# Graph hops and attention: the edge counts of the front moved ahead of the first table and onto TensorE

## The chip, the cores and the metric

The kernel runs on one core of one Trainium2 chip. The metric is the device time of one execution in microseconds, lower is better. The engines are named as the profile names them: PE is TensorE (PEld its weight loads), DVE is VectorE, ACT is ScalarE, POOL is GpSimd, SP is SyncE, which here only issues DMAs. PSUM is the memory that PE accumulates into; DVE and ACT read it back.

## The reference, cut to what matters

There are N = 10000 nodes with D = 128 features and E = 160000 edges. Seven times the features are spread along the edges; then each node attends over its eight versions of itself.

```python
h = x
toks = [x]
for _ in range(7):
    msg = h[src] * deg_inv_sqrt[src, None] * deg_inv_sqrt[dst, None]
    h = segment_sum(msg, dst, N)
    toks.append(h)
tok = jnp.stack(toks, axis=1)          # (N, 8, D)
# layernorm, q/k/v, softmax over the 8 tokens, wo, residual,
# layernorm, softmax of r @ w_r over the tokens, weighted sum -> (N, D)
```

The graph comes as two unsorted lists of edge ends, `src` and `dst`. Before a hop can be done with matmuls, the edges must be sorted into blocks of destination nodes. That sorting, and the first scaled table of node features, is the front of the kernel, and it is what the change touches.

## The kernel before, in words

**Order of the whole.** `Hops.run` (L525) calls `first_table` (L162), `pass_a` (L231) and `decode` (L286), then builds the matrices of the blocks while it does the first hop, does the six further hops, and the attention follows. A scheduler places the instructions: each engine executes its own list in a fixed order, and the list is not always the order of the source. Engines wait for each other by semaphores only.

**The first table.** `first_table` loads x (5.1 MB) with DMAs issued by ACT (L170, L171) into the buffer `tab` number 1, multiplies 79 tiles of rows by 1/sqrt(degree) on ACT (L173), takes the largest magnitude of all of it with one DVE reduction `mc` (L176), finds a power of two from it through a small chain of PE and DVE steps (`pow2`, `colmax`, `spread`), and writes table 0 as two 16-bit halves: the high half on ACT (L152) and the rest on DVE (L153), in four pieces of 20 tiles. Each piece is stored to DRAM.

**Sorting by destination block.** `pass_a` lays the 160000 edges out as 128 partitions x 1250 columns. `key` is the destination's block (dst >> 7, 79 values), `d1` and `d2` hold the other digits of the edge. The columns are 25 chunks of B = 50. Inside a chunk each edge needs its rank among the edges of its partition with the same key. `lag` (L213) counts, for each edge, the equal keys ahead of it in its chunk: for each distance l from 1 to 49 one DVE comparison writes `eq` (L219) and one DVE addition adds it to `wl` (L220), so the 98 instructions depend on each other in a chain through `wl` and one `eq` buffer.

Then for each chunk: `oh`, a one-hot of the keys (DVE, L189); `U`, 50 matmuls that count the keys of the partitions before (PE, L263); `U2`, its copy (ACT, L270); `ux` = oh x U2 (DVE, L202); `R`, 17 matmuls that pick out the offsets and add `wl` (PE, L206 and L207); `rk`, the rank (DVE, L210); `o12`, two products of oh with d1 and d2 (DVE, L195; the trace shortens the name to `o`, and `oh`, `rob` and `R` of other places also come from L189 and L195); `ro`, a one-hot of the ranks (DVE, L278); `ta`, 50 matmuls that put the edges' values in their place (PE, L283); and `TT`, the sum of ta's two halves (DVE, L284). `oh`, `U2`, `rk` and `ro` have two buffers, `U`, `R` and `ta` two in PSUM, `ux` and `o12` one. `count` for the next chunk is called before the rank of this one, so `oh` and `U` run one chunk ahead.

**Decoding.** `decode` unpacks TT into keys, sources and destinations with DVE and ACT operations on 128 x 2000 elements, scales TT on DVE (L307), and `lag_rows` (L222) counts equal keys `kB` again, now along the 25 chunks: 24 comparisons (L228) and 24 additions to `wB` (L229). After that `place` begins the next sorting step with two one-hots, `ur` matmuls (L336) and their copies.

Of the kernel before, what the change touches and what calls it, by code (L numbers as in the profile page):

```python
# [7 lines left out]
F32 = mybir.dt.float32  # L8
F16 = mybir.dt.float16
# [4 lines left out]
ALU = mybir.AluOpType  # L14
# [23 lines left out]
class Hops:  # L38
    def __init__(self, ctx, dp, missing, tc, x, src, dst, dis):
# [36 lines left out]
        V.memset(self.ones16, 1.0)  # L76
        self.iof = cp.tile([128, 128], F32, name="iof")
# [84 lines left out]
    def first_table(self):  # L162
        nc, V, A = self.nc, self.nc.vector, self.nc.scalar
        tab0 = self.tab[0]
        y = self.tab[1].bitcast(F32)
        nc.gpsimd.memset(y[:, NT - 1:, :], 0.0)
        nc.gpsimd.memset(tab0[:, NT:, :], 0.0)
        h = NT // 2
        for a, b in ((0, h), (h, NT - 1)):
            nc.scalar.dma_start(y[:, a:b, :], self.x[a * 128:b * 128, :].rearrange("(t p) d -> p t d", p=128))  # L170
        nc.scalar.dma_start(y[:N - (NT - 1) * 128, NT - 1, :], self.x[(NT - 1) * 128:, :])  # L171
        for t in range(NT):
            A.activation(y[:, t, :], y[:, t, :], AF.Copy, scale=self.disT[:, t:t + 1])  # L173
        with self.tc.tile_pool(name="ft", bufs=1) as sp, self.tc.tile_pool(name="ftp", bufs=1, space=PSUM) as pp:
            mc = sp.tile([128, 1], F32, name="mc")
            V.tensor_reduce(mc, y[:, :NT, :], axis=mybir.AxisListType.XY, op=ALU.max, apply_absolute_value=True)  # L176
            q = self.pow2(pp, sp, mc, 2.0 ** 40)
            V.tensor_copy(self.sinv, q[:, 1:2])
            for a in range(0, NT, 20):
                b = min(NT, a + 20)  # L180
                self.to_table(y[:, a:b, :], tab0, q[:, 0:1], a, b)
                self.rows(0, tab0, a, b, nc.sync)
        V.tensor_scalar(self.ctok[0], self.disT, self.sinv, None, op0=ALU.mult)
# [29 lines left out]
    def lag(self, ep, key, w, a, m):  # L213

        V = self.nc.vector
        V.memset(w, 0.0)
        for l in range(1, m):
            eq = ep.tile([128, a, m], F16, name="eq")
            V.tensor_tensor(eq[:, :, l:], key[:, :, l:], key[:, :, :m - l], op=ALU.is_equal)  # L219
            V.tensor_add(w[:, :, l:], w[:, :, l:], eq[:, :, l:])  # L220

    def lag_rows(self, ep, key, w, m):  # L222

        V = self.nc.vector
        V.memset(w, 0.0)
        for l in range(1, m):
            eq = ep.tile(list(key.shape), F16, name="eq")
            V.tensor_tensor(eq[:, l:], key[:, l:], key[:, :m - l], op=ALU.is_equal)  # L228
            V.tensor_add(w[:, l:], w[:, l:], eq[:, l:])  # L229

    def pass_a(self):  # L231
        tc, nc, V, A, T, G = self.tc, self.nc, self.nc.vector, self.nc.scalar, self.nc.tensor, self.nc.gpsimd
        with ExitStack() as c:
# [5 lines left out]
            with tc.tile_pool(name="pe", bufs=1) as ep:  # L239
# [12 lines left out]
                self.lag(ep, key.rearrange("p (c b) -> p c b", b=B), wl, NCH, B)  # L252
# [12 lines left out]

            st = count(0)
            for ch in range(NCH):
                oh, U = st
                U2 = wp.tile([128, NK, 2], F16, name="U2")
                A.activation(U2, U[:, :, None].to_broadcast([128, NK, 2]), AF.Copy)  # L270
                if ch + 1 < NCH:
# [7 lines left out]
                                self.io2[:, None].to_broadcast([128, NP, 128, 2]), op=ALU.is_equal)  # L279
                ta = pp.tile([128, 2, NK], F32, name="ta")  # L280
# [3 lines left out]
                V.tensor_reduce(self.TT[:, ch, :NK], ta.rearrange("p h k -> p k h"), axis=X, op=ALU.add)  # L284

    def decode(self):  # L286
# [3 lines left out]
        with tc.tile_pool(name="pd", bufs=1) as ep:  # L290
# [16 lines left out]
            V.tensor_scalar(self.TT, self.TT, 1024.0, -1023.0, op0=ALU.mult, op1=ALU.add)  # L307
            self.lag_rows(ep, self.kB, self.wB, NCH)
# [216 lines left out]
    def run(self, ctx, nhop=K):  # L525
        tc, nc, V, A, T, G = self.tc, self.nc, self.nc.vector, self.nc.scalar, self.nc.tensor, self.nc.gpsimd
        with ExitStack() as c:
# [3 lines left out]
            self.first_table()  # L531
# [626 lines left out]
```

## Time and profile before

| | us |
|---|---|
| median of 3 runs | 4419.87 (4418.78 to 4421.31) |
| the profiled execution | 4388.44 |
| its span, from first to last record | 4386.5 |
| busy: PE, DVE, ACT, POOL | 3836.6, 3383.4, 2453.6, 1680.0 |
| mean granted PE clock | 0.963 |

The profile is of one execution. Its own time is 31.4 us under the median of the runs, so its span and the median are not compared with each other; a difference between two profiles is compared with a difference between two medians. The front takes the first 560 us of the span. In the answers that list stretches of time, a row gives the stretch, its length, the busy time of PE, PEld, DVE, ACT and POOL with the number of instructions, then the granted PE clock (1.00 is full speed), the busy share of the DMA engines and GB/s. In the rows of the timeline the numbers are the start, the time that the group covers, the engine, the line, the operation, what is written and from what, and how many; in brackets stands how long the engine had been idle before, and what ended that.

### The profile page before, as it was taken

The numbers are of one execution on the slowest core, as the hardware profiler recorded it, in microseconds if no ns is written. First come the engines' busy times: TensorE is split into PE (matmuls) and PEld (weight loads), VectorE is DVE, ScalarE is ACT, GpSimd is POOL, SyncE is SP. The second block draws the span as 40 slices with busy tenths as digits, with TensorE's granted clock in tenths as the row PEclk, the third lists the DMA queues.
The fourth block names the chain that finished last, engine by engine and source line by source line (L and its number), as shares of the span: only waits on it lengthen the run. The fifth ranks groups of instructions, "written<-read, shape, count | busy, mean of one in ns | idle before, by whom it ended". The sixth has DMA issues, their size and how long they took to land.

```text
span 4386.5 us, 162053 instructions
## 1 busy us (share of the span) xinstructions
PE 3836.6 (87%) x69456; PEld 3003.0 (68%) x69456; DVE 3383.4 (77%) x6923; ACT 2453.6 (56%) x5989; POOL 1680.0 (38%) x1898
## 2 busy tenths in 40 slices
PE   0466379999997999999999999999999998999997
PEld 0466366666665777777777777777777776788875
DVE  5888899999995677666666666666765554899998
ACT  3000036666565666566566656656665555988885
POOL 0000023333333555555455545545555553222222
PEclk9887689999998999999999999999999998999998
DMA  4000034444445555555555555555555555122220
GB/s 122 1 1 1 1 108 152 149 153 149 143 155 180 182 181 188 170 184 183 175 184 179 184 173 184 181 176 180 183 185 167 170 170 151 54 78 78 77 72 19
DMA packets 320607, 594.73 MB, mean 136 GB/s; under 512 B 55623, under 2 KB 213541, under 8 KB 314629
## 3 DMA queue, kind: packets, MB, share of 16 engines
q1 hardware_dynamic: 219749, 477.37, 34.1%
q0 software_dynamic: 35392, 72.55, 5.4%
q10 hardware_dynamic: 64736, 34.38, 2.8%
q8 instruction: 544, 8.91, 0.8%
q14 instruction: 186, 1.52, 0.1%
HBM read 455.43 MB, written 128.67 MB: 133 GB/s over the span
## 4 chain that ended last, share of the span: by engine, by line
PE 56%; ACT 6%; DVE 3%; issue 1%; DMA 1%; SPq 0%; another core or an unknown queue 0%; ACTq 0%; DVEq 0%; POOLq 0%
PE acc L468 21%; PE p L492 20%; ACT eb L495 5%; PE acc L454 3%; PE pv L842 3%; PE po L853 3%; PE pu L831 3%; PE pt L821 1%; DVE eb L495 1%; PE ps L873 1%; PE pf L1021 1%; PE sm L879 1%; DMA og<-tabh,oidx 1%; DVE st L948 0%; SPq L734 0%
## 5 line engine op out<-in xcount | busy, mean ns | idle before, releaser
L495 ACT CAST eb<-p 128x512 f16<-128x512 f32 x3081 | 1598.5, 600 | 935.5 <-PE p L492 878.9
L495 DVE CAST eb<-p 128x512 f16<-128x512 f32 x1896 | 1180.7, 683 | 570.9 <-PE p L492 531.4
L492 PE MATMUL p<-tab,w 128*32 128x256 f16 x39816 | 1437.7, 275 | 111.1 <-ACT eb L495 35.1
L492 PEld LDWEIGHTS <-w 128*32 128x32 fp8e4 x39816 | 974.1, 96 | 491.4 <-issue 400.7
L468 PE MATMUL acc<-eb,w 128*128 128x256 f16 (+1 forms) x9954 | 1244.5, 274 | 13.1 <-DVE indeg L544 8.8
L439 POOL DMA_INDIRECT og<-tabh,oidx x553 | 631.9, 1143 | 1628.7 <-PE acc L454 868.7
L468 PEld LDWEIGHTS <-w 128*128 128x128 fp8e4 x9954 | 954.6, 98 | 174.6 <-issue 59.6
L439 POOL DMA_INDIRECT og<-tabd,oidx x541 | 557.4, 1030 | 457.5 <-PE acc L481 276.3
L521 POOL TENSOR_SCALAR r<-s,ctok 128x128 f32<-128x128 f32 x474 | 297.4, 627 | 40.0 <-DVE s L483 25.5
L627 DVE SCALAR_TENSOR_TENSOR tab<-s,c,tab 128x128 f16<-128x128 f32 x395 | 140.8, 356 | 183.1 <-ACT tab L626 182.1
L626 ACT ACTIVATE tab<-s,c 128x128 f16<-128x128 f32 x395 | 158.6, 401 | 166.0 <-DVE s L483 157.5
L483 DVE TENSOR_REDUCE s<-acc 128x128 f32<-128x256 f32 x553 | 228.5, 413 | 25.4 <-PE acc L481 18.8
L867 ACT ACTIVATE junk<-x 128x128 f32<-128x128 f32 x625 | 245.0, 394 | 0.0
L270 ACT ACTIVATE U<-U 128x158 f16<-128x158 f32 x25 | 7.6, 303 | 378.6 <-PE U L263 378.6
L429 DVE TENSOR_TENSOR w<-dsl,iof 128x2432 fp8e4<-128x2432 f16 x79 | 211.8, 2681 | 0.0
L283 PE MATMUL ta<-o,ro 128*128 128x158 f16 x1250 | 127.2, 278 | 90.5 <-DVE ro L278 90.5
L853 PEld LDWEIGHTS po<-v,pT 128*128 128x128 f32 x1250 | 160.1, 194 | 43.7 <-issue 26.7
L283 PEld LDWEIGHTS <-ro 128*128 128x128 f16 x1250 | 122.1, 119 | 94.5 <-DVE ro L278 94.2
L842 PE MATMUL pv<-Wv,xT 128*128 128x131 f32 x1250 | 175.6, 284 | 3.7 <-ACT xT L822 3.1
L853 PE MATMUL po<-v,pT 128*128 128x128 f32 x1250 | 167.7, 278 | 7.0 <-DVE o L859 7.0
L925 POOL TENSOR_TENSOR p<-e,in 128x512 f32<-128x512 f32 (+1 forms) x40 | 40.8, 1021 | 342.0 <-DVE e L923 342.0
L842 PEld LDWEIGHTS pv<-Wv,xT 128*128 128x128 f32 x1250 | 153.3, 192 | 20.2 <-issue 8.3
(267 smaller groups left out, 4509.1 us busy)
## 6 DMA issues: line engine op xcount, KB each, us to landing
w<-gsd SPq DMA_DIRECT2D x474, 592.0 KB
gsd<-w SPq DMA_DIRECT2D x79, 592.0 KB
rb<-srow SPq DMA_DIRECT2D x79, 576.0 KB
tok<-r SPq DMA_DIRECT2D x546, 64.0 KB
x<-tok SPq DMA_DIRECT2D x266, 128.0 KB
tabd<-tab ACTq DMA_DIRECT2D x395, 64.0 KB
og<-tabh,oidx POOLq DMA_INDIRECT x553
og<-tabd,oidx POOLq DMA_INDIRECT x541
```

The lines of the kernel that those rows point to most:

```text
L283: T.matmul(ta, ro[:, j, :, i], o12[:, j, :, i], start=j + i == 0, stop=j + i == NP)
L429: V.tensor_tensor(w[:, :NJ * 128].rearrange("p (j d) -> p j d", d=128), dsl[:, g, :, None].to_broadcast([128, NJ, 128]), self.iof1[:, None ...
L439: self.nc.gpsimd.indirect_dma_start(out=o, out_offset=None, in_=src[0] if i == NI else src[1], in_offset=bass.IndirectOffsetOnAxis(ap=self ...
L468: T.matmul(acc[0][:, :m], w[:, J * 128:(J + 1) * 128], e[:, j, :m], start=first and J == 0, stop=J == NG - 1 and not (first or late))
L483: V.tensor_reduce(s, acc[0][:, 0:256].rearrange("p (h d) -> p d h", h=2), axis=X, op=ALU.add)
L492: T.matmul(p[32 * q:32 * q + 32, j], w[:, NJ * 128 + s * CAP:NJ * 128 + (s + 1) * CAP], tab[:, s, :], start=True, stop=True)
L495: (A.copy if evac(jj) else V.tensor_copy)(e[:, :n, 0:256], p[:, :n].rearrange("p j h d -> p j (h d)"))
L521: self.nc.gpsimd.tensor_scalar(r, s, ct[:, t:t + 1], None, op0=ALU.mult)
L626: A.activation(new[:, t, 0:128], s, AF.Copy, scale=c1[:, t:t + 1])
L842: T.matmul(p[:, g - a, :], S[i]["xT"][:, g, :], Wv, start=True, stop=True)
L853: T.matmul(p[:, g - a, :], PT[i % 2][:, g, :], S[i]["v"][:, g, :128], start=True, stop=True)
L867: A.activation(j, S[i]["x"][:, g, :], AF.Square, bias=S[i]["x"][:, g, 0:1], scale=-1.0, accum_out=S[i]["sq"][:, g:g + 1])
```

## The change

The change is in the front alone.

- `first_table` is split. `first_rows` (loading x, scaling its rows) is now called inside `pass_a`, behind the unpacking of the edges; the rest of `first_table` (reduction, power of two, table 0, stores) is called when the loop over chunks comes to chunk 2.
- `lag` and `lag_rows` no longer add on DVE. DVE only compares, into three rotating `eq` buffers. PE adds: a matmul with the identity `id16` as weights adds each `eq` to a sum `W` in PSUM (one to three, or up to five, banks; a first matmul with zeros clears each), and ACT copies `W` to `wl` or `wB` at the end.
- The sum `TT` of a chunk is issued one chunk later (`take(ch - 1, ta)`), after the next chunk's `rk` and `ro` in the source.
- TT's scaling in `decode` goes from DVE to ACT.

```diff
+        self.zero16 = cp.tile([128, 512], F16, name="zero16")
+        V.memset(self.zero16, 0.0)
...
-    def first_table(self):
+    def first_rows(self):
...
         for t in range(NT):
             A.activation(y[:, t, :], y[:, t, :], AF.Copy, scale=self.disT[:, t:t + 1])
+
+    def first_table(self):
+        nc, V = self.nc, self.nc.vector
+        tab0, y = self.tab[0], self.tab[1].bitcast(F32)
         with self.tc.tile_pool(name="ft", bufs=1) as sp, self.tc.tile_pool(name="ftp", bufs=1, space=PSUM) as pp:
...
-    def lag(self, ep, key, w, a, m):
+    def lag(self, ep, pp, key, w, a, m):
-        V = self.nc.vector
-        V.memset(w, 0.0)
+        V, T, n = self.nc.vector, self.nc.tensor, 512 // m
+        W = pp.tile([128, -(-a // n), 512], F32, name="W")
+        parts = [(b, b * n, min(a, b * n + n)) for b in range(W.shape[1])]
+        out = lambda b, r: W[:, b, :r * m].rearrange("p (a m) -> p a m", m=m)
+        for b, r, e in parts:
+            T.matmul(W[:, b, :(e - r) * m], self.id16, self.zero16[:, :(e - r) * m], start=True, stop=False, skip_group_check=True)
         for l in range(1, m):
             eq = ep.tile([128, a, m], F16, name="eq")
             V.tensor_tensor(eq[:, :, l:], key[:, :, l:], key[:, :, :m - l], op=ALU.is_equal)
-            V.tensor_add(w[:, :, l:], w[:, :, l:], eq[:, :, l:])
+            for b, r, e in parts:
+                T.matmul(out(b, e - r)[:, :, l:], self.id16, eq[:, r:e, l:], start=False, stop=l == m - 1, skip_group_check=True)
+        for b, r, e in parts:
+            self.nc.scalar.copy(w[:, r:e, :], out(b, e - r))
...
-    def lag_rows(self, ep, key, w, m):
+    def lag_rows(self, ep, pp, key, w, m):
...
             V.tensor_tensor(eq[:, l:], key[:, l:], key[:, :m - l], op=ALU.is_equal)
-            V.tensor_add(w[:, l:], w[:, l:], eq[:, l:])
+            for b, r, e in parts:
+                r1 = max(r, l * k)
+                if r1 < e:
+                    T.matmul(W[:, b, r1 - r:e - r], self.id16, flat(eq)[:, r1:e], start=False, stop=(l + 1) * k >= e,
+                             skip_group_check=True)
+        for b, r, e in parts:
+            self.nc.scalar.copy(flat(w)[:, r:e], W[:, b, :e - r])
...
-            with tc.tile_pool(name="pe", bufs=1) as ep:
+            with tc.tile_pool(name="pe", bufs=1) as ep, tc.tile_pool(name="peq", bufs=3) as eqp, \
+                    tc.tile_pool(name="pW", bufs=1, space=PSUM) as pw:
...
-                self.lag(ep, key.rearrange("p (c b) -> p c b", b=B), wl, NCH, B)
+                self.first_rows()
+                self.lag(eqp, pw, key.rearrange("p (c b) -> p c b", b=B), wl, NCH, B)
...
+            def take(ch, ta):
+                V.tensor_reduce(self.TT[:, ch, :NK], ta.rearrange("p h k -> p k h"), axis=X, op=ALU.add)
+
             st = count(0)
             for ch in range(NCH):
+                if ch == 2:
+                    self.first_table()
...
+                if ch:
+                    take(ch - 1, ta)
                 ta = pp.tile([128, 2, NK], F32, name="ta")
...
-                V.tensor_reduce(self.TT[:, ch, :NK], ta.rearrange("p h k -> p k h"), axis=X, op=ALU.add)
+            take(NCH - 1, ta)
...
-            V.tensor_scalar(self.TT, self.TT, 1024.0, -1023.0, op0=ALU.mult, op1=ALU.add)
-            self.lag_rows(ep, self.kB, self.wB, NCH)
+            A.activation(self.TT, self.TT, AF.Copy, scale=1024.0, bias=-1023.0)
+            self.lag_rows(eqp, pw, self.kB, self.wB, NCH)
...
-            self.first_table()
             self.pass_a()
```

The scheduler moves more than the source shows. Rows below are in the order in which an engine executes them; a row names the line, the operation, the tile written, the tiles read, and the size; line numbers are each kernel's own (an operation at L219 before stands at L229 after).

First place: DVE's list around the reduction `mc` of the first table (`m`, `r` and `q` are the small chain to the power of two, `tab_230` and `tab_231` tables 0 and 1). Before, first the middle of the table's chain and then the start of the count:

```order
L147 TENSOR_SCALAR q_359<-q_359 128x1
L178 COPY sinv<-q_359 128x1
L183 TENSOR_SCALAR ctok_235<-disT,sinv 128x79
L153 SCALAR_TENSOR_TENSOR tab_230<-tab_231,q_359,tab_230 128x20x128 x3
L153 SCALAR_TENSOR_TENSOR tab_230<-tab_231,q_359,tab_230 128x19x128
L216 MEMSET wl 128x625
L249 TENSOR_SCALAR it<-ed 128x1250
L219 TENSOR_TENSOR eq<-key 128x25x49
L250 TENSOR_TENSOR it<-it 128x1250
L220 TENSOR_TENSOR wl<-wl,eq 128x25x49
```

Now, the end of the count and what follows it on DVE (`tab_233` is table 1):

```order
L229 TENSOR_TENSOR eq<-key 128x25x2
L229 TENSOR_TENSOR eq<-key 128x25
L195 TENSOR_TENSOR oh<-key,io_214 128x3950 x2
L201 TENSOR_TENSOR o_766<-oh,d_264 128x25x158
L201 TENSOR_TENSOR o_766<-oh,d_265 128x25x158
L182 TENSOR_REDUCE mc<-tab_233 128x1
L208 TENSOR_TENSOR ux<-oh,U_689 128x3950
L127 TENSOR_REDUCE m_966<-pm 1x1
L195 TENSOR_TENSOR oh<-key,io_214 128x3950
L143 TENSOR_SCALAR r_968<-m_966 1x1
```

The whole count and two chunks' `oh` with one chunk's products now stand ahead of `mc`, and the chain behind it is mixed with the chunks 0 to 2.

Second place: DVE's list in the middle of the loop over chunks. Before, one of the two patterns that take turns there:

```order
L278 TENSOR_TENSOR ro<-rk,io_212 128x6400
L189 TENSOR_TENSOR oh<-key,io_212 128x3950
L202 TENSOR_TENSOR ux<-oh,U_882 128x3950
L284 TENSOR_REDUCE TT<-ta 128x79
L195 TENSOR_TENSOR o_959<-oh,d_385 128x25x158
L195 TENSOR_TENSOR o_959<-oh,d_386 128x25x158
L210 TENSOR_REDUCE rk<-R 128x50
```

Now, the same in every chunk:

```order
L309 TENSOR_TENSOR ro<-rk,io_214 128x6400
L195 TENSOR_TENSOR oh<-key,io_214 128x3950
L208 TENSOR_TENSOR ux<-oh,U_1397 128x3950
L201 TENSOR_TENSOR o_1474<-oh,d_264 128x25x158
L201 TENSOR_TENSOR o_1474<-oh,d_265 128x25x158
L216 TENSOR_REDUCE rk<-R 128x50
L293 TENSOR_REDUCE TT<-ta 128x79
```

`TT` stood between `ro` and the products; it now stands behind `rk`. In its place the first product waits for the last `ta` matmul of the chunk before, because `o12` has one buffer. PE's list is now, chunk by chunk, `ta`, `U`, `R`.

Third place: the head of ACT's list (`tab_231` before and `tab_233` now are table 1, `U_614` and `U_689` the first U2). Before:

```order
L170 DMA tab_231<-in_x 128x39x128 x2
L171 DMA tab_231<-in_x 16x128
L173 ACT_TABLE_LOAD
L173 ACTIVATE tab_231<-tab_231,disT 128x128 x79
L152 ACTIVATE tab_230<-tab_231,q_359 128x20x128 x3
```

Now:

```order
L172 DMA tab_233<-in_x 128x39x128
L270 ACT_TABLE_LOAD
L270 CAST key<-it 128x1250
L172 DMA tab_233<-in_x 128x39x128
L272 ACTIVATE d_264<-it 128x1250
L173 DMA tab_233<-in_x 16x128
L175 ACTIVATE tab_233<-tab_233,disT 128x128 x5
L276 ACTIVATE d_265<-it 128x1250
L175 ACTIVATE tab_233<-tab_233,disT 128x128 x74
L233 CAST wl<-W 128x500 x2
```

The key is made between the two large DMAs of x, and the copies of `W` stand behind all 79 scalings. From the first one-hot of `place` on, every engine's list is the same as before, and POOL's and SP's lists are the same from the first row.

More of the change, by code (lines that the diff above doesn't have):

```diff
@@ L160, in rows @@
             eng.dma_start(o.rearrange("(t p) w -> p t w", p=128), tab[:, a:t1, :])
-    def first_table(self):
-        nc, V, A = self.nc, self.nc.vector, self.nc.scalar
+    def first_rows(self):
+        nc, A = self.nc, self.nc.scalar
         tab0 = self.tab[0]
@@ L219, in lag @@
             V.tensor_tensor(eq[:, :, l:], key[:, :, l:], key[:, :, :m - l], op=ALU.is_equal)
-            V.tensor_add(w[:, :, l:], w[:, :, l:], eq[:, :, l:])
-    def lag_rows(self, ep, key, w, m):
-        V = self.nc.vector
-        V.memset(w, 0.0)
+            for b, r, e in parts:
[3 more added lines that the diff above has]
+    def lag_rows(self, ep, pp, key, w, m):
+        V, T, k = self.nc.vector, self.nc.tensor, key.shape[2]
+        n = 512 // k * k
+        W = pp.tile([128, -(-m * k // n), 512], F32, name="W")
+        flat = lambda z: z.rearrange("p m k -> p (m k)")
+        parts = [(b, b * n, min(m * k, b * n + n)) for b in range(W.shape[1])]
+        for b, r, e in parts:
+            T.matmul(W[:, b, :e - r], self.id16, self.zero16[:, :e - r], start=True, stop=False, skip_group_check=True)
         for l in range(1, m):
@@ L228, in lag_rows @@
             V.tensor_tensor(eq[:, l:], key[:, l:], key[:, :m - l], op=ALU.is_equal)
-            V.tensor_add(w[:, l:], w[:, l:], eq[:, l:])
+            for b, r, e in parts:
[3 more added lines that the diff above has]
+                             skip_group_check=True)
+        for b, r, e in parts:
+            self.nc.scalar.copy(flat(w)[:, r:e], W[:, b, :e - r])
     def pass_a(self):
@@ L289, in decode @@
         self.kB, self.sl, self.dl, self.wB = (bp.tile([128, NCH, NTP], F16, name=n) for n in ("kB", "sl", "dl", "wB"))
-        with tc.tile_pool(name="pd", bufs=1) as ep:
+        with tc.tile_pool(name="pd", bufs=1) as ep, tc.tile_pool(name="pdq", bufs=3) as eqp, \
+                tc.tile_pool(name="pdW", bufs=1, space=PSUM) as pw:
             vi = ep.tile([128, NCH, NTP], I32, name="vi")
```

## The prediction

> **What bounds the kernel now.** I read the span and the engines' busy times first, then stretches of the front, then what DVE waited for, then the timeline where a term needed a duration. Stretches: total length, then busy PE, PEld, DVE, ACT, POOL, then clock.
>
> ```profile
> span 4386.5 us, 162053 instructions
> ...
> 0.00:76.90 76.90, 1.32 (x4) 0.76 (x4) 32.41 (x47) 36.05 (x88) 5.23 (x24) 1.00 0.44 134
> 76.90:130.98 54.08, 0.00 (x0) 0.00 (x0) 50.68 (x100) 1.74 (x2) 0.00 (x0) 1.00 0.19 56
> 130.98:500.04 369.06, 236.16 (x2925) 221.63 (x2925) 313.88 (x175) 7.57 (x25) 0.00 (x0) 0.81 0.00 1
> 500.04:513.40 13.36, 0.00 (x0) 0.00 (x0) 13.29 (x11) 3.74 (x2) 0.00 (x0) 0.56 0.00 0
> 513.40:547.69 34.29, 0.00 (x0) 0.00 (x0) 32.57 (x50) 0.00 (x0) 0.00 (x0) 0.50 0.00 0
> 547.69:560.24 12.55, 6.90 (x46) 5.69 (x47) 6.74 (x4) 0.57 (x2) 0.00 (x0) 0.65 0.00 0
> 560.24:4386.50 3826.26, 3592.18 (x66481) 2774.94 (x66480) 2933.82 (x6540) 2403.92 (x5871) 1674.77 (x1874) 0.98 0.48 152
> ```
>
> The six stretches of the front are: first table; count of equal keys; 25 chunks; decoding; second count; start of `place`. From 76.90 on DVE is busy nearly all the time or waits for PE. In both counts PE does nothing, so 54.08 and 34.29 us are pure DVE chains. After 560 us PE is busy 94% of the time; every engine's list from the start of `place` on is unchanged, so I take what the front saves as a shift of all that follows.
>
> What DVE waits for, in total, times, longest:
>
> ```profile
> DVE mc L176 <- ACT tab L173: 33.5, 1, 33.5
> ...
> DVE TT L284 <- PE ta L283: 55.2, 25, 5.9
> ```
>
> DVE sits idle 33.5 us for ACT to scale x, and 55.2 us in the chunks for `ta`. These two and the additions are what the change is aimed at.
>
> ```profile
> L219 DVE TENSOR_TENSOR eq<-key 128x1225 f16<-128x1225 f16 (+48 forms) x49 | 24.8, 505 | 1.7
> L220 DVE TENSOR_TENSOR wl<-wl,eq 128x1225 f16<-128x1225 f16 (+48 forms) x49 | 24.5, 501 | 1.6
> L228 DVE TENSOR_TENSOR eq<-kB 128x1920 f16<-128x1920 f16 (+23 forms) x24 | 16.3, 678 | 0.8
> L153 DVE SCALAR_TENSOR_TENSOR tab<-tab,q,tab 128x2560 f16<-128x2560 f32 (+1 forms) x4 | 11.1, 2847 | 1.9 <-ACT tab L152 1.9
> ```
>
> **The front up to the last chunk.** I follow DVE's new list in time.
>
> ```profile
> 2.19 12.61 ACTq L170 DMA_DIRECT2D tab<-in_x  x1
> 6.31 0.81 DVE L244 TENSOR_SCALAR it<-ed 128x1250 int32<-128x1250 int32 x1 [5.17 <-DMA ed<-in_dst]
> 13.77 0.89 DVE L225 MEMSET wB<- 128x1000 uint32 x1 [0.28 <-DVE triw L72]
> 24.95 23.17 ACT L173 ACTIVATE tab<-tab,disT 128x128 f32<-128x128 f32 x79
> 48.16 10.69 DVE L176 TENSOR_REDUCE mc<-tab 128x1 f32<-128x10112 f32 x1 [33.45 <-ACT tab L173]
> 76.15 1.24 ACT L247 ACTIVATE d<-it 128x1250 f16<-128x1250 int32 x1
> 77.74 1.45 DVE L250 TENSOR_TENSOR it<-it 128x1250 int32<-128x1250 int32 x1
> ```
>
> The edges are unpacked by 13.77 already; one unpacking step of some 0.7 us moves ahead, so the first comparison starts near 14.5. The 49 comparisons cost 24.8 busy. They no longer depend on each other, so their gaps go (1.7), but with three `eq` buffers the fourth waits for PE to have added the first. I take 24.8 and 1.45 for the unpacking step between them: 40.7. Bounds of the 24.8: 20 if neighbours overlap by 0.09 each as two products do (4.33 for two of 2.21, quoted below), 27 if PE at half clock sets the pace (the 49 distances have 25 x 1225 = 30625 columns; 16 x 250 columns take 3.32 at half clock, a row below, so 25.4). Then two `oh` and two products.
>
> The middle of the chunks, one pattern:
>
> ```profile
> 408.74 4.18 PE L283 MATMUL ta<-o,ro 128*128 128x158 f16 x50 [0.48 <-DVE ro L278]
> 421.16 2.21 DVE L189 TENSOR_TENSOR oh<-key,io 128x3950 f16<-128x3950 f16 x1
> 421.30 6.19 PE L283 MATMUL ta<-o,ro 128*128 128x158 f16 x50 [6.50 <-DVE ro L278]
> 423.29 2.21 DVE L202 TENSOR_TENSOR ux<-oh,U 128x3950 f16<-128x3950 f16 x1
> 427.53 0.32 DVE L284 TENSOR_REDUCE TT<-ta 128x79 f32<-128x158 f32 x1 [2.03 <-PE ta L283]
> 427.77 4.33 DVE L195 TENSOR_TENSOR o<-oh,d 128x3950 f16<-128x3950 f16 x2
> 432.02 0.41 DVE L210 TENSOR_REDUCE rk<-R 128x50 f16<-128x250 f32 x1
> 432.35 2.20 DVE L189 TENSOR_TENSOR oh<-key,io 128x3950 f16<-128x3950 f16 x1
> 434.47 3.48 DVE L278 TENSOR_TENSOR ro<-rk,io 128x6400 f16<-128x6400 f16 x1
> ```
>
> From start to start, `oh` takes 2.13, `ux` the same, the products 4.25, `rk` 0.33, `TT` 0.24, `ro` 3.40 (3.48 less the overlap): 12.5 us of DVE per chunk, against 369.06 / 25 = 14.8 now. Two `oh` and two products are 8.5, so DVE reaches `mc` at 49.2. ACT's scalings ended at 48.1; in the new list they follow the same DMA issues, the table load is out of the way earlier (1.3), one more 1.24 step is between them. So the 33.5 us wait is gone and `mc` ends at 59.9. Its cover is thin: the second DMA of x is now issued behind `key`, which needs the edges (6.31 + 0.81, and 1.24 for a cast of that size: 8.4) instead of at 2.19. If its 12.61 us of issue are its own work, and not time until earlier packets drain, the scalings and `mc` come up to 8 us late; I take nothing, since the first DMA of the same size had been issued by 2.19, and keep the 8 for the range. Sending the `wl` copies behind the scalings delays `U` to about 50, beside `mc`, at no cost.
>
> From 59.9, DVE has left: 25 x 12.5 - 8.5 = 304.0 for the chunks, 11.1 for the table, some 1.5 for the small chain: 376.5 without a wait. Waits: about 1.5 for the first `rk` (its `R`, 3.32 at half clock, has only one `oh` of 2.1 beside it), 1 for the chain's PE step behind chunk 1's `ta`, 5.9 at the end for the last `TT` as now. And a new one. `TT` no longer waits, but the next instruction that needs the same `ta` does: the first product overwrites `o12`, which `ta` reads, and has one buffer. Behind it on DVE are `rk`, `TT`, `ro`; PE waits for `ro`. The product is reached 4.25 after `ro`; `ta` starts 0.14 after it (421.16, 421.30) and takes 4.18 to 6.19, depending on the clock. I take the middle, 5.2, and 0.15 for the release: 5.5, so 1.2 us of wait, 22 times: 26.4. Bounds: 0.2 and 2.2. `R` of the same chunk then ends about when the products do.
>
> Sum: 376.5 + 1.5 + 1 + 5.9 + 26.4 = 411.3 for the end of the chunks, 500.04 before: 88.7 saved.
>
> Why `ta` is slow, in stretches as long as the clock's steps (PE busy is the second number, the clock the third from the right):
>
> ```profile
> 167.25:170.67 3.42, 2.05 (x21) 1.54 (x18) 3.42 (x4) 0.30 (x1) 0.00 (x0) 1.00 0.03 5
> 170.67:174.08 3.41, 1.50 (x39) 1.50 (x40) 3.41 (x2) 0.00 (x0) 0.00 (x0) 1.00 0.01 2
> 174.08:177.49 3.41, 2.47 (x28) 2.29 (x26) 3.41 (x2) 0.30 (x1) 0.00 (x0) 0.50 0.00 0
> 177.49:180.91 3.42, 3.42 (x28) 3.42 (x27) 0.56 (x1) 0.00 (x0) 0.00 (x0) 0.50 0.00 0
> 180.91:184.32 3.41, 2.97 (x31) 2.47 (x29) 2.29 (x2) 0.00 (x0) 0.00 (x0) 1.00 0.03 5
> ```
>
> 2.05 us of work in a stretch keep the full clock, 1.50 lose it; at half clock 2.47 do not bring it back, 3.42 do. In the new loop PE idles while DVE does `rk`, `TT` and `ro`: about 4.3 us in each chunk, which two stretches cannot share without one of them falling under 1.7. So the clock falls once a chunk, in the gap, and `ta` starts at half. A chunk of 12.5 + 1.2 = 13.7 is then also four such stretches, 13.65, so the pattern should repeat itself.
>
> The Trainium skill, page "TensorE: Matmul & The Clock Gate", Part 1 on the clock gate, has the clock fall after a whole idle window of some 3.4 us on a free-running grid. By that alone a 4.3 us gap would hold a whole window in only a quarter of the positions, and most chunks would keep the full clock. The row with 1.50 us of work followed by 0.50 speaks against it; rival 1 below has that outcome.
>
> **Decoding, the second count, the start of `place`.**
>
> ```profile
> 512.29 1.20 DVE L307 TENSOR_SCALAR TT<-TT 128x2000 f32<-128x2000 f32 x1
> ...
> 549.88 3.28 PE L336 MATMUL ur<-oh,id 128*128 128x152 f16 x25 [50.20 <-DVE oh L189]
> 556.38 3.32 PE L206 MATMUL ur<-ux,id 128*128 128x250 f16 x16 [2.55 <-DVE ux L202]
> 560.26 1.80 PE L336 MATMUL ur<-oh,id 128*128 128x152 f16 x25 [0.51 <-DVE rk L210]
> 565.44 1.86 PE L206 MATMUL ur<-ux,id 128*128 128x250 f16 x16 [0.23 <-DVE ux L202]
> ```
>
> TT's scaling leaves DVE (1.2; ACT is idle there, and `place` needs TT only 40 us later). The second count goes from 34.29 to its comparisons, 16.3 + 0.8, plus 0.5 for a first stall on a PE that comes from idling: 17.6, so 16.7 saved; it has 24000 columns, 19.9 us at half clock, so 3 less if the clock never rose. PE now comes to `place` warm: the first `ur` and `R` could take 1.80 and 1.86 instead of 3.28 and 3.32, 2.9 in all; but five copies of `W` on ACT stand ahead, four of 480 columns (25 copies of 158 took 7.57, 0.3 each, so up to 0.9 for 480, up to 4 in all), and only the first `oh`, 2.1, lies beside them. I take 1.5, between -1 and 2.9. Sum 19.4.
>
> **The total** is 88.7 + 19.4 = 108.1. The profiled execution would go from 4388.4 to 4280.3. Its time lies 31.4 under the median of the runs; the difference goes onto the median: 4419.9 - 108.1 = 4312.
>
> **The rivals.**
> 1. The clock stays full through the gaps; the products never wait. For it: 2.05 us of work in a stretch held it. Against: the 4.3 us gap. 26.4 less: 4285.
> 2. The wait only changes its name: `ta` runs at half clock nearly whole, as at 421.30, and the product waits 2.2 in every chunk. 22 us more: 4334. For it: 6.19 occurs in every second pair of chunks. Against: those came after 6.5 us of idling.
> 3. Slower. PE's adding becomes the bound: the operands are shifted slices of 25 short runs each, a form that the trace does not show. If such columns streamed slowly, DVE would wait for `eq` buffers in both counts. It decides from 24.8 + 17.6 + 108 = 150 us of PE for 54625 columns, 2.75 ns a column; the slowest row of a 16-bit matmul here is 0.83 (3.32 / 4000). At 3 ns: 164 us, 14 over, 4434.
>
> **How the numbers follow.** Forecast 0.63 (it spans 4302 to 4324 with x late by 8 or the counts at half clock), rival 1 0.13, rival 2 0.17, rival 3 0.03, and 0.04 that something later takes back over half. The range 4284 to 4338 takes in the first two rivals. A measurement of this kernel can tell about 0.2%, 9 us. Faster 0.95, same 0.02, slower 0.03.
>
> **What would show it.** Right: DVE with no wait over 3 us ahead of `mc`; the chunks ending near 411; a wait of about 1.2 us in front of the first product, on `ta`, and none at `TT`; the second count near 18 us; the stretch from 560.24 to the end still 3826 long. Wrong: `eq` waiting for PE through the count, a wait of 2 us or none in the chunks, `mc` waiting for ACT by 8, or hops that got longer.

## The result, and the profile after

The changed kernel takes 4307.96 us (median of 4 runs, 4306.16 to 4308.57); the kernel before took 4419.32 beside it. The ratio is 0.9747, 95% interval 0.9735 to 0.9758: 111 us saved (107 to 117 by that interval), against 108.1 forecast and a forecast time of 4312. The profiled execution of after took 4306.16 us.

The stretches of the front again, in the profile of after: the first unpacking, the first count, two chunks with the first table among them, the other 23 chunks, the decoding, the second count, the start of `place`, and the rest. Columns: stretch, its length, busy PE, PEld, DVE, ACT, POOL, the clock.

```profile
0.00:14.18 14.18, 1.60 (x4) 0.69 (x5) 7.75 (x31) 2.54 (x4) 5.47 (x24) 1.00 0.89 300
14.18:36.95 22.77, 20.54 (x144) 12.85 (x144) 22.21 (x52) 14.77 (x45) 0.22 (x2) 1.00 0.56 153
36.95:102.08 65.13, 32.22 (x410) 29.51 (x407) 62.09 (x37) 22.37 (x49) 0.00 (x0) 0.81 0.12 34
102.08:406.92 304.84, 199.82 (x2524) 188.57 (x2524) 274.29 (x155) 6.34 (x21) 0.00 (x0) 0.86 0.04 13
406.92:419.29 12.37, 1.02 (x5) 0.51 (x6) 12.27 (x10) 5.50 (x3) 0.00 (x0) 0.69 0.00 0
419.29:435.10 15.81, 14.49 (x80) 7.72 (x80) 14.56 (x25) 0.07 (x1) 0.00 (x0) 0.81 0.00 0
435.10:446.18 11.08, 5.43 (x46) 4.20 (x46) 6.75 (x5) 2.57 (x7) 0.00 (x0) 0.85 0.01 1
446.18:4304.40 3858.22, 3625.41 (x66481) 2773.72 (x66480) 2935.53 (x6540) 2402.59 (x5871) 1673.32 (x1874) 0.98 0.49 151
```

The chunks end at 406.92 instead of 500.04. The point where `place` goes on with its second `ur` product, 560.26 before, is now 446.18: the front is 114.1 us shorter. Both counts now have PE at work (20.54 and 14.49 us) beside a DVE that is busy nearly throughout. The rest took 3858 us here and 3826 in the profiled execution of before, which had itself run 31 us under the timed runs of its kernel. The same instructions stand there in both; what that stretch takes when nothing is changed is the first experiment.

What DVE waits for in after, up to the end of the front (total, times, longest):

```profile
DVE o L201 <- PE ta L316: 25.3, 21, 3.2
DVE TT L293 <- PE ta L316: 5.2, 1, 5.2
...
DVE rk L216 <- PE ur L213: 3.5, 1, 3.5
DVE mc L182 <- ACT tab L175: 1.8, 1, 1.8
```

The 33.5 us ahead of `mc` are 1.8. The 55.2 us ahead of `TT` are 5.2, the last chunk's. In their place stands the wait that the prediction named: the first product on `ta`, 21 times, 25.3 us in all. The timeline of the front shows what the idle time was filled with (start, length, engine, operation, idle time before it and what ended it):

```profile
7.58 7.03 ACTq L172 DMA_DIRECT2D tab<-in_x  x1
...
22.48 14.51 DVE L229 TENSOR_TENSOR eq<-key 128x1000 f16<-128x1000 f16 x40
...
26.03 21.72 ACT L175 ACTIVATE tab<-tab,disT 128x128 f32<-128x128 f32 x74
...
41.62 4.33 DVE L201 TENSOR_TENSOR o<-oh,d 128x3950 f16<-128x3950 f16 x2
...
47.79 10.69 DVE L182 TENSOR_REDUCE mc<-tab 128x1 f32<-128x10112 f32 x1 [1.84 <-ACT tab L175]
```

While ACT scales x (to 47.75), DVE does its 49 comparisons, two one-hots and two products. The scalings end 0.4 earlier than before: the second DMA of x, issued at 7.58 instead of 2.19, was done at 14.61, where it had been done at 14.80. So at least 5.6 of its 12.61 us in before were not its own work; what it waited for was not looked up.

The steady loop of after, one chunk in the timeline (PE rows and the product that waits):

```profile
114.68 5.28 PE L316 MATMUL ta<-o,ro 128*128 128x158 f16 x50 [4.91 <-DVE ro L309]
...
119.80 2.09 PE L289 MATMUL U<-oh,tri 128*128 128x79 f16 x50
120.00 4.34 DVE L201 TENSOR_TENSOR o<-oh,d 128x3950 f16<-128x3950 f16 x2 [1.12 <-PE ta L316]
```

PE has nothing for 4.91 us, `ta` then takes 5.28, and the product stands 1.12 until `ta` lets go of `o12`. `U` behind it takes 2.09. In the next chunk, where `ta` starts at 128.35, the clock reads 0.50 from 128.30 to 130.00 and 1.00 from 132.00 on: it is low at the start of `ta` and back before `U`.

### The profile page after: what moved, and what is told of

It reads as the page before. It is cut to its first block, busy times and chain, and to the rows that moved or that the text cites. A ratio compares the mean times of both kernels' runs of the same rounds, so it can differ in the third digit from the quotient of the medians.

```text
span 4304.4 us, 162521 instructions
## 1 busy us (share of the span) xinstructions
PE 3900.5 (91%) x69691; PEld 3017.8 (70%) x69691; DVE 3335.4 (77%) x6848; ACT 2456.8 (57%) x5998; POOL 1679.0 (39%) x1898
## 4 chain that ended last, share of the span: by engine, by line
PE 59%; ACT 6%; DVE 3%; issue 1%; DMA 1%; SPq 0%; another core or an unknown queue 0%; ACTq 0%; POOLq 0%; DVEq 0%; POOL 0%
PE acc L502 21%; PE p L526 21%; ACT eb L529 5%; PE acc L488 4%; PE pv L875 3%; PE po L886 3%; PE pu L864 3%; PE pt L854 1%; PE ps L906 1%; PE pf L1054 1%; DVE eb L529 1%; PE sm L912 1%; DMA og<-tabh,oidx 0%; SPq L767 0%
## 5 line engine op out<-in xcount | busy, mean ns | idle before, releaser
L526 PE MATMUL p<-tab,w 128*32 128x256 f16 x39816 | 1465.4, 275 | 105.5 <-ACT eb L529 34.2
L316 PEld LDWEIGHTS <-ro 128*128 128x128 f16 x1250 | 125.4, 121 | 115.4 <-DVE ro L309 108.1
```

Of the source, the lines that this page charges most:

```text
L316: T.matmul(ta, ro[:, j, :, i], o12[:, j, :, i], start=j + i == 0, stop=j + i == NP)
L526: T.matmul(p[32 * q:32 * q + 32, j], w[:, NJ * 128 + s * CAP:NJ * 128 + (s + 1) * CAP], tab[:, s, :], start=True, stop=True)
```

## The experiments

In all diffs lines start with + or - against the kernel named. "Front" is the time from the first instruction to the second `ur` product of `place` (560.26 in before, 446.18 in after), read in each profile; it repeats to about a microsecond, while the time of the whole differs between chips. "The copy of after" is the second profile of after, with a front of 446.73. The first set of four ran beside a before of 4155.62 us, the second beside 4393.08, the third beside 4394.21; differences are taken inside a set.

**Before, unchanged** (no edit).

> The kernel before, unchanged, against itself. All theories: the ratio holds 1.000, within 0.002 either way. What it is for is the profile: that of before spans 4386.5 us, 31 us under its own timed runs (4418 to 4421), and that of after runs the stretch behind the second ur matmul in 3858 us where before's took 3826. Theory A (the change leaves that stretch alone, and before's profiled execution was a quick one there): a second profile of before spans about 4415 to 4419, its second ur matmul stands at 560 again and the stretch behind takes about 3855 to 3860. Theory B (the change costs some 31 us in the hops): the stretch behind the second ur matmul takes 3826 again, and the span is near 4387.

Measured: ratio 1.0001 (0.9991 to 1.0011), 4156.0 us. Its two stretches, the front and what lies behind (columns as above):

```profile
0.00:559.56 559.56, 247.75 (x2976) 231.49 (x2976) 449.68 (x384) 49.65 (x118) 5.23 (x24) 0.82 0.08 25
559.56:4157.60 3598.04, 3438.53 (x66481) 2804.64 (x66480) 2936.14 (x6540) 2395.37 (x5871) 1672.22 (x1874) 0.98 0.53 161
```

Neither theory had this: the front is the same to 0.7 us, 559.56, but the stretch behind took 3598 us instead of 3826, with the same numbers of instructions, DVE as busy as ever (2936) and PE 154 us less busy (3438.53 against 3592.18). So the length of that stretch differs from chip to chip or from one execution to the next with nothing changed. Theory B asked for 3826 again and falls with it as it stood; the 32 us between the two first profiles cannot be put down to the change.

**After, unchanged** (no edit; in the second set).

> The kernel after, unchanged, beside the kernel before on this chip. The second profile of before (another chip or time) spanned 4157.6 us with the front as it was: first comparison 76.6, last sum of values 499.1, second product of the placement at 559.4; only the stretch behind took 3598 us instead of 3826. Theory A (the change acts in the front alone and what lies behind differs from chip to chip): the front of this run repeats to within a microsecond (chunks end near 406.9, second product of the placement near 446), and the time is 109 to 114 us under that of before here, whatever before takes (ratio 0.9725 to 0.9755). Theory B (the change shortens the whole run in proportion): 2.5% of before here.

```profile
446.73:4275.80 3829.07, 3603.79 (x66481) 2776.08 (x66480) 2935.05 (x6540) 2402.07 (x5871) 1669.53 (x1874) 0.98 0.49 152
```

Measured: 4277.60 us, ratio 0.9736 (0.9722 to 0.9749), 115.5 us under before in this set. The front is 446.73, which is 112.8 under that of the control above. The stretch behind took 3829 us, what the first profile of before had. Theory A holds on the mechanism: the front moves, by 113 to 114 us, and what follows shifts with it. The saving in time, 115.5 with an interval of some 6 us either way, lies just above the 109 to 114 expected. By its time alone theory B (2.5% of 4393 is 110 us) stands at the edge of that interval; the first set speaks against it, since three variants of the front below left the stretch behind at 3587 to 3597 beside before's 3598.

**One part alone: the sum one chunk behind.** Against before:

```
+            def take(ch, ta):
+                V.tensor_reduce(self.TT[:, ch, :NK], ta.rearrange("p h k -> p k h"), axis=X, op=ALU.add)
+
...
+                if ch:
+                    take(ch - 1, ta)
                 ta = pp.tile([128, 2, NK], F32, name="ta")
...
-                V.tensor_reduce(self.TT[:, ch, :NK], ta.rearrange("p h k -> p k h"), axis=X, op=ALU.add)
+            take(NCH - 1, ta)
```

> Before, with one part of the change alone: a chunk's values are summed one chunk behind. Clock theory: the wait of the sum on its own products goes (2.0 us a chunk), but the first product then waits for ta, since the chunk's TensorE work falls to half clock over the gap in front of ta and the loop locks to four stretches of 3.413 us; the period goes from 14.5 us to 13.65, some 23 times 0.85, so 20 us less: about 4399 (ratio 0.9955). Rival 1 (no clock in it, the vector engine alone sets the period of 12.46): about 45 us less, 4374 (0.990). Rival 2 (the new wait eats the whole of the old one): 4419 (1.000).

Measured: 4136.75 us, 18.9 under before, ratio 0.9953 (0.9936 to 0.9970); front 540.90, 18.7 shorter. What DVE waits for in it:

```profile
DVE o L195 <- PE ta L288: 30.2, 24, 3.2
...
DVE TT L267 <- PE ta L288: 5.2, 1, 5.2
```

55.2 us of waits at `TT` (54.5 in the control of this set) became 30.2 + 5.2 = 35.4, most of it at another instruction: 19.8 less, or 19.1 against the control, which is about the gain. The clock theory expected 20 us; rival 1 (45) and rival 2 (0) fall.

**One part undone: the table first.** Against after:

```
-                self.first_rows()
                 self.lag(eqp, pw, key.rearrange("p (c b) -> p c b", b=B), wl, NCH, B)
...
-                if ch == 2:
-                    self.first_table()
...
+            self.first_rows()
+            self.first_table()
             self.pass_a()
```

> After, with the first table made in front of everything as before; the sums of equal keys stay on TensorE and the sum of a chunk's values stays one chunk behind. Theory of the parts: the vector engine stands idle for the table's rows again (it did so for 44 of the first 74 us in before) and the first comparison starts at about 76 to 77 instead of 14.2; of the 62 us in between, 26 are the table's own work, which leaves the chunks. So 34 to 37 us slower than after, about 4343 (ratio to before 0.983). Rival (filling the idle time bought little, because the same loads and the same vector work lie there either way, and the gain is that of the additions and the loop): under 10 us slower than after, about 4312 (0.976).

Measured: 4081.80 us, ratio to before 0.9825 (0.9807 to 0.9843); front 487.80, 41.1 longer than the copy of after. Its DVE waits (those of after stand above):

```profile
DVE mc L182 <- ACT tab L175: 33.7, 1, 33.7
DVE o L201 <- PE ta L313: 29.1, 24, 3.2
...
DVE tab L155 <- ACT tab L154: 1.9, 1, 1.9
DVE it L274 <- ACT key L270: 1.4, 1, 1.4
...
DVE q L134 <- PE pb L133: 0.7, 1, 0.7
...
DVE m L127 <- PE pm L125: 0.6, 1, 0.6
```

The rival (under 10) falls. The parts' theory was 4 to 7 us short, and the rows say where: 33.7 against 1.8 at `mc` is 31.9; the small waits around the table, which in after are filled with chunk work, are 1.9 + 1.4 + 0.7 + 0.6 = 4.6; and 29.1 against 25.3 at the products is 3.8 (3.4 against the copy's 25.7), three more chunks that wait. The sum is 40.3 of 41.1; DVE's busy time in the front is 1.4 longer too (401.42 against 400.00 in the copy).

**One part undone: the additions on DVE again.** Against after, in both counts (the first is shown; the second likewise):

```
-        W = pp.tile([128, -(-a // n), 512], F32, name="W")
...
+        V.memset(w, 0.0)
         for l in range(1, m):
             eq = ep.tile([128, a, m], F16, name="eq")
             V.tensor_tensor(eq[:, :, l:], key[:, :, l:], key[:, :, :m - l], op=ALU.is_equal)
-            for b, r, e in parts:
-                T.matmul(out(b, e - r)[:, :, l:], self.id16, eq[:, r:e, l:], start=False, stop=l == m - 1, skip_group_check=True)
-        for b, r, e in parts:
-            self.nc.scalar.copy(w[:, r:e, :], out(b, e - r))
+            V.tensor_add(w[:, :, l:], w[:, :, l:], eq[:, :, l:])
```

> After, with the additions of equal keys back on the vector engine in both counts (49 in the first, 24 in the second); the order of the table and of the chunk's sums stays. Theory of the parts: the first count grows by its 49 additions, 25 us by the rows of before, of which the 1.8 us wait for the first rows is taken up; the second count goes from 15.8 back to 34.3, 18.5 us. Together about 40 us slower than after, 4348 (ratio to before 0.984). Rival 1 (the additions would have been hidden in the wait for the first rows, so TensorE bought only the second count): about 18 us slower than after, 4326 (0.979). Rival 2 (the comparisons paced by TensorE lose as much as the additions took): no slower than after, 4308 (0.975).

Measured: 4098.69 us, ratio to before 0.9860 (0.9843 to 0.9877); front 499.52, 52.8 longer than the copy of after. DVE groups of the first count in it (busy, mean ns, idle before), one of its waits, and then the comparisons of both counts in after:

```profile
L225 DVE TENSOR_TENSOR eq<-key 128x1225 f16<-128x1225 f16 (+48 forms) x49 | 24.7, 504 | 1.3
L226 DVE TENSOR_TENSOR wl<-wl,eq 128x1225 f16<-128x1225 f16 (+48 forms) x49 | 24.5, 500 | 1.4
```

```profile
DVE o L201 <- PE ta L298: 29.4, 24, 3.2
```

```profile
L229 DVE TENSOR_TENSOR eq<-key 128x1225 f16<-128x1225 f16 (+48 forms) x49 | 21.0, 502 | 0.6 <-PE W L231 0.4
L246 DVE TENSOR_TENSOR eq<-kB 128x1920 f16<-128x1920 f16 (+23 forms) x24 | 14.6, 676 | 0.9 <-PE W L250 0.9
```

Both rivals fall. The parts' theory was 13 us short, in three places. It let the additions fill the wait ahead of `mc`, but the scheduler put `mc` into the middle of the count (at 47.80), and that wait stayed (1.7). Taking the additions away saves more than the additions' own time: a comparison that is followed by another one overlaps it, so 49 of them cover 21.0 us instead of 24.7, though each still lasts 0.50. (Whether it is the missing dependence or the like neighbour that lets them overlap was not tried apart.) The first count's saving is 24.7 + 1.3 + 24.5 + 1.4 - 21.0 - 0.6 = 30.3, not 25. And 29.4 us of product waits instead of 25.3 (24 instead of 21 of them) are 4.1 more. With 18.5 for the second count (34.31 from the first comparison's start to the first one-hot of `place`, 452.89 to 487.20, against 15.81 in the copy of after) the sum is 52.9, or 52.5 with the copy's 25.7 us of product waits, against 52.8 measured.

The three parts undone or done alone give 18.7 + 41.1 + 52.8 = 112.6 us of front; the whole change gave 112.8. The parts add, though not each wait by itself: the three more chunks that wait (3.8 and 4.1 us) stand in both of the last two sums, so an agreement to 0.2 us is in part chance.

**Why the product waits: the buffer.** Against after:

```
-                o12 = w1.tile([128, NP, 2 * NK, 2], F16, name="o12")
+                o12 = wp.tile([128, NP, 2 * NK, 2], F16, name="o12")
...
-                ro = wp.tile([128, NP, 128, 2], F16, name="ro")
+                ro = w1.tile([128, NP, 128, 2], F16, name="ro")
```

> After, with the products (o12) in two buffers and the one-hots of ranks (ro) in one, so that no product waits for the ta of the chunk before it; the vector engine's order comes out in pairs of chunks instead of single chunks. Buffer theory (the 25.3 us of waits exist because o12 has one buffer; with two they go): 20 to 25 us faster than after, ratio to after 0.9945 to 0.995. Clock theory (TensorE falls to half clock over the gap in front of ta, and with U, R and ta at half clock a chunk is 3.3 + 3.5 + 6.4 us of TensorE or its locked mix; the wait only changes its place, to the one-hots' buffer or the sum): within 5 us of after.

Measured: 4249.33 us, 28.3 under after, ratio to before 0.9669 (0.9656 to 0.9682); front 418.93. The clock in the chunks (120 to 370 us), and one pair of chunks in the timeline:

```profile
120.00:370.00 250.00, 175.08 (x2300) 161.44 (x2298) 248.73 (x140) 5.75 (x19) 0.00 (x0) 0.89 0.00 1
```

```profile
216.83 3.81 PE L316 MATMUL ta<-o,ro 128*128 128x158 f16 x50 [1.33 <-DVE ro L309]
217.01 4.34 DVE L201 TENSOR_TENSOR o<-oh,d 128x3950 f16<-128x3950 f16 x2
221.26 3.49 DVE L309 TENSOR_TENSOR ro<-rk,io 128x6400 f16<-128x6400 f16 x1
224.66 0.32 DVE L293 TENSOR_REDUCE TT<-ta 128x79 f32<-128x158 f32 x1
224.81 6.37 PE L316 MATMUL ta<-o,ro 128*128 128x158 f16 x50 [4.16 <-DVE ro L309]
```

The clock theory's expectation, that the wait would only change its place, is wrong. The clock still falls (0.89 on average; the `ta` at 224.81 takes 6.37 us), and DVE is busy all the same, 248.73 of 250 us: the products of 217.01 start 0.18 after `ta` began to read the other buffer. The front is 27.8 us shorter than the copy's, somewhat more than the 20 to 25 of the buffer theory: DVE is idle for 25.7 us less and busy for 2.1 less (397.94 against 400.00). This is the first of the versions here that beat both kernels.

**Why the product waits: the clock.** Against after, matmuls whose sum nobody reads, between the ranks and `ta`:

```
+            fp = c.enter_context(tc.tile_pool(name="fill", bufs=1, space=PSUM))
+            fill = fp.tile([128, 250], F32, name="fill")
...
+                for _ in range(22):
+                    T.matmul(fill.rearrange("p (j i k) -> p j i k", i=2, k=5), self.id16, rk[:, :, :, None].to_broadcast([128, NP, 2, 5]),
+                             start=True, stop=True, skip_group_check=True)
```

> After, with 22 matmuls of 128x250 added to each chunk between the ranks and ta, on an own PSUM tile that nobody reads; they start when rk is there and take 2.75 us at full clock (16 of the same shape take 2.04 us in after). They put work into the 4.6 us in which TensorE has none. Clock theory: no stretch of 3.413 us is left with under 1.64 us of work, TensorE stays at full clock, ta starts no later and ends before the first product needs it; the period goes from 13.65 to 12.46 us (the vector engine's own work), 18 to 22 us faster than after (ratio to after about 0.995), the product waits fall from 25 us to under 3. Buffer or order theory (the wait is of the order of the work, not of the clock): TensorE has more to do, nothing is gained, 0 to 5 us slower.

```profile
120.00:370.00 250.00, 212.89 (x2794) 186.31 (x2792) 250.00 (x141) 6.04 (x20) 0.00 (x0) 1.00 0.01 1
```

Measured: 4258.06 us, 19.5 under after, ratio to before 0.9690 (0.9676 to 0.9703); front 425.65. More work on PE made the kernel faster: the clock is 1.00, DVE busy for 250.00 of 250 us, the period 12.46 us. `ta` takes 3.80 us there. So the clock theory is right about why `ta` is long; the buffer decided whether that is felt. The product waits did not fall under 3 us, as expected, but to 6.3, in three chunks, 3.91 of it in one while the table is made. These 6.3 us are about what this front has over that of the two buffers (425.65 against 418.93).

**Half of the filling.** The same with `range(11)`.

> The same with 11 added matmuls a chunk, 1.4 us at full clock. Clock theory with its threshold (full clock is kept by a stretch of 3.413 us with at least about 1.64 us of work and lost by one with 1.50 or less, as the rows of before and after show): 11 don't fill the stretch, TensorE falls all the same, the period stays at four stretches, 13.65 us; 0 to 5 us slower than after. Rival (the clock follows the share of work, or only a wholly idle stretch lets it fall): half of the gain of 22 or all of it, 9 to 22 us faster than after.

Measured: 4279.07 us, ratio 0.9738 (0.9724 to 0.9751), 1.5 over after; front 448.14, period 13.65 to 13.73. PE in the timeline of it, in the gap of one chunk (idle time before each in brackets), and then two stretches of its PE at the start of `ta` (length, busy PE, clock):

```profile
208.02 1.56 PE L308 MATMUL fill<-rk,id 128*128 128x250 f16 x11 [0.93 <-DVE rk L216]
211.66 4.55 PE L321 MATMUL ta<-o,ro 128*128 128x158 f16 x39 [2.07 <-DVE ro L314]
```

```profile
211.60:213.00 1.40, 1.34 (x14) 0.70 0.00 0
213.00:215.00 2.00, 2.00 (x18) 0.50 0.00 0
```

PE is never idle for longer than 2.07 us here, and the clock falls all the same, at about 212. The rival, which expected 9 to 22 us, falls in both its forms. The rule of the Trainium skill that the prediction weighed (page "TensorE: Matmul & The Clock Gate", Part 1: the clock falls after a wholly idle window of some 3.4 us) does not cover this: no such window exists in these rows.

**Between the two: 15 and 18.** The same with `range(15)` and `range(18)`, in the third set.

> After with 15 added matmuls a chunk (11 left the period at 13.65 us and the clock at 0.88, 22 brought 12.46 and 0.98). A model of the loop from the rows, in which a stretch of 3.413 us with under 1.6 us of TensorE work loses full clock, puts the step between 14 and 15: period 12.46, all of the gain, as with 22 (about 20 us under after, ratio to before 0.969). If the gain follows the amount of added work: about 7 us of the 20 (4 of the 11 matmuls between), ratio 0.972.

> After with 18 added matmuls a chunk. Step: all of the gain, period 12.46, about 20 us under after (ratio to before 0.969). In proportion: 7 of 11 between 11 and 22, about 13 us under after, ratio 0.9708, a period between 12.46 and 13.65.

```profile
120.00:370.00 250.00, 195.05 (x2652) 172.51 (x2649) 248.23 (x141) 6.04 (x20) 0.00 (x0) 1.00 0.01 1
```

```profile
212.63 2.07 PE L308 MATMUL fill<-rk,id 128*128 128x250 f16 x15 [1.19 <-DVE rk L216]
216.26 3.80 PE L321 MATMUL ta<-o,ro 128*128 128x158 f16 x50 [1.56 <-DVE ro L314]
```

Measured: 4250.97 us with 15 (ratio 0.9672, 0.9656 to 0.9688; front 422.38; rows above) and 4252.57 with 18 (0.9679, 0.9663 to 0.9695; front 425.21). A step, not a proportion: 1.56 us of work in the gap bring nothing, 2.07 bring the clock to 1.00, `ta` to 3.80 and the period to 12.46.

**Both at once.** The two buffers and the 22 matmuls.

> After with both: the products in two buffers (and the one-hots of ranks in one), and 22 added matmuls a chunk. Theory 1 (the wait of the products took two things together, a ta at half clock and one buffer that showed it; with either gone the vector engine's own 12.46 us a chunk are the bound): nothing on top of the two buffers alone, ratio to before 0.966 to 0.969, 24.9 us for a pair of chunks, though TensorE now stands at full clock. Rival (the clock and the buffer are two gains of their own, which add): 15 to 20 us under the two buffers alone, ratio about 0.9625.

```profile
120.00:370.00 250.00, 212.89 (x2772) 186.10 (x2770) 250.00 (x141) 6.05 (x20) 0.00 (x0) 1.00 0.01 1
```

Measured: 4248.43 us, ratio 0.9666 (0.9650 to 0.9682), front 418.62, against 0.9669 and 418.93 for the two buffers alone. Nothing on top: the two are not gains of their own. A `ta` at half clock and a single buffer made the wait together, and either cure leaves DVE's own 12.46 us a chunk in the middle of the loop.

## Why the prediction was right, step by step

The mechanism came as forecast: the front got shorter, what follows was shifted, and one new wait appeared where it was expected. By the profiles the front is 114.1 us shorter, 6.0 more than the 108.1 of the sum; the terms below say where. The time itself, with its interval of some 5 us either way, cannot tell the two apart.

- **First comparison at 14.5:** 14.18.
- **The 49 comparisons, 24.8 + 1.45:** the mis-sized term. They took 22.77 with the unpacking step (14.18 to 36.95), so 21.3 without. The bound of 20, from products that overlap by 0.09, was the nearer row; the comparison's own row in before came from a list in which an addition that needs it follows each one. PE at half clock did not set the pace: the clock was 1.00 and DVE waited 0.4.
- **No wait at `mc`, `mc` ends at 59.9:** a wait of 1.84, since DVE came 3.2 earlier than the 49.2 of the sum (after the products, at 45.95); `mc` ended at 58.48. The bound of 8 us for a late x did not come: that DMA's issue was shorter the later it started.
- **The new wait, 1.2 us x 22 = 26.4:** 25.3 in 21, and the period 13.65 as worked out. The first rival (full clock) would have needed more work in the gap: 1.56 us of filling were too little, 2.07 enough; the second (2.2 in every chunk) did not occur.
- **Chunks end at 411.3:** 406.92. Of the 4.4 us, 3.5 are the comparisons; the last `TT` (5.2 for 5.9) and the product waits (25.3 for 26.4) give 1.8 more, and the wait at `mc` takes 1.8 back; the rest, 0.9, is the net of small terms: the start 0.3 earlier, the first `rk` (0.8 for 1.5), no wait in the table's small chain (1 forecast), and about 1 us more of busy time and small waits.
- **Second count 17.6:** 15.81, for the same reason as the first: 14.6 of comparisons instead of 16.3. TT's scaling, 1.2 in the sum, gave 1.0 (decoding 12.37 for 13.36).
- **`place` 1.5 less:** 11.08 against 12.55, the right sum from other parts, as the rows of after show:

```profile
435.03 2.08 ACT L253 CAST wB<-W 128x480 f16<-128x480 f32 x5 [16.02 <-PE W L250]
...
437.29 1.81 PE L370 MATMUL ur<-oh,id 128*128 128x152 f16 x25 [2.30 <-DVE oh L195]
...
442.31 3.33 PE L212 MATMUL ur<-ux,id 128*128 128x250 f16 x16 [2.54 <-DVE ux L208]
```

  The copies took 2.08, all hidden beside the one-hot. The first `ur` was quick (1.81 for 3.28); `R`, behind 2.54 us of idling, was at half clock as before (3.33 for 3.32).
- **The third rival, PE's adding as the bound:** 20.54 us for the first count's 30625 columns are 0.67 ns a column, and 14.49 for the second's 24000 are 0.60, far from the 2.75 from which it would have decided. Only the first count reads the shifted slices in many short pieces; in the second each slice is one long run. Whether the short pieces cost anything cannot be read from this, since DVE set the pace: it waited 0.4 us for PE in the first count and 0.9 in the second.
- **The rest unchanged:** in its instructions and its busy DVE yes; its length differs by chip, 3587 to 3598 in the first set for before and three variants alike, 3829 to 3837 in the second for after and its variants. The prediction's way of carrying the 31.4 us between profile and runs over to the median was right in effect, not because it was understood. The traces show where PE's time differs. The 39816 matmuls of the hops that write `p`, with weights of 128 x 32, kept PE busy for 1283 to 1285 us in the four profiles of the first set, and for 1442 to 1445 in the seven of the other two; the 9954 that write `acc`, with weights of 128 x 128, took 1239 to 1247 in all of them. Of the 33 us of PE between the two first profiles 27.7 are in `p` too (1437.7 and 1465.4). Why `p` differs stays open.

## What to carry to other kernels

Follow the limiting engine's list through the new order and price an instruction by what stands behind it there: taking away the dependent partner of each of a row of instructions can save more than the partner took (30.3 us here for 24.5 of additions). A wait that is removed hands its cause on to the next user of the same buffer, so ask which buffer shows it next: one more copy of `o12`, paid with one of `ro`, was worth 28 us, no less than keeping the clock up. Where PE works in bursts inside a loop of another engine, count its work in each 3.413 us: here 1.56 us of it in the gap left the burst behind at 5.3 us, and 2.07 brought it to 3.80.

## What the runs showed of the hardware

The clock falls on too little work, not only on none: with idle times no longer than 2.07 us it fell (11 added matmuls, 1.56 us of work in the gap), and it held with 2.07 us of work and idle times of 1.19 and 1.56. From these two alone it could also be one idle time of some 2 us that lets it fall. A place in the trace of before, behind the front, speaks against that (length, busy PE, clock, in two neighbouring stretches of 3.41 us):

```profile
1338.02:1341.43 3.41, 1.49 (x7) 1.00 0.01 2
1341.43:1344.84 3.41, 0.04 (x4) 0.50 0.85 286
```

The seven small matmuls of the first stretch are 1.49 us of work, and no idle time up to its end is longer than 1.29 us; still the clock is at 0.50 in the next. How much work keeps the clock is only bounded: 1.50 us lost it and 2.05 kept it in the rows that the prediction quotes.

The loop, as long as DVE waits for PE in it, takes on the rhythm of the clock's steps. In after the sums of consecutive chunks come every 13.65 us, four steps of 3.413. In before four chunks made a pattern; in the control's timeline:

```profile
340.59 0.32 DVE L284 TENSOR_REDUCE TT<-ta 128x79 f32<-128x158 f32 x1 [2.03 <-PE ta L283]
...
398.62 0.32 DVE L284 TENSOR_REDUCE TT<-ta 128x79 f32<-128x158 f32 x1 [2.04 <-PE ta L283]
```

From 340.59 to 398.62 are 58.03 us, seventeen steps of 3.413. With the sum alone one chunk behind, in the copy of after and with half of the filling the chunks first came every 13.67 to 13.73 us and then settled at 13.65. So the gain of a shortened step need not be the step's length here: the period went from 58.03 / 4 = 14.5 to 13.65, and to 12.46 where DVE no longer waited. That no period between these would settle was not tried.

The same 66481 matmuls behind the front kept PE busy for 3429 to 3439 us in the first set and 3597 to 3604 in the other two, at a clock of 0.98 to 0.99 in each; nearly all of the difference is in one of their forms, the `p` matmuls named above. A saving is better read in the part of the profile that the change touches than in the time of the whole.
